# Block 0's feed-forward with VectorE in program order, and the last two groups' second layer inside the first pair of products

## The chip, the core and the metric

One NeuronCore of a Trainium2 chip runs the whole program. TensorE multiplies matrices into PSUM, VectorE and ScalarE work elementwise, GpSimd does a few subtractions and SyncE issues most DMA transfers. Each engine takes its own instructions in the order in which they stand, and semaphores join the engines. The metric is the device time of one execution in microseconds; lower is better.

## The reference, cut to what matters

```python
x = attention(q, k, v)                        # 8 batches of 576 tokens, chunks of 64 -> 4608 tokens of 512
gate = sigmoid(causal_depthwise_conv(x, conv_w))
y = (gate * (x @ w_val)) @ w_out              # 512 x 512 each
mu, var = y.mean(-1), y.var(-1)
xn = (y - mu) / sqrt(var + 1e-6) * g_ln
out = y + relu(xn @ w_ch1) @ w_ch2            # 512 x 2048 and 2048 x 512
```

The weights arrive as float64, and a matmul takes fp32r operands (fewer bits than f32), so a weight is decoded from its bit pattern to f32 and then split into a high and a low part; a product is high*high + high*low + low*high.

## The kernel before

The 4608 tokens are nine blocks of 512. Attention, gate and the two projections of all blocks come first, in an order that a planner writes out. Then comes the feed-forward, whose hidden 2048 columns are 16 groups f of 128. Block 0's feed-forward is done directly, group by group, while the weights are still being decoded; blocks 1 to 8 follow in pairs of blocks, by a scheme of 7 products in place of 8 (`ff_pair`, one call for each pair of groups; "pair 0" below is its first call, for groups 0 and 1 of blocks 1 and 2).

Block 0's part is a loop over f. `ff1(0, f)` is the first layer: 12 matmuls (`psh`, L219), then ScalarE's relu writes the high half `hh` (L646) and VectorE the low half `hl` (L647). PSUM holds two `psh` tiles, so ff1(f) can't begin before `hl` of group f-2 has been read out. `ff2` is the second layer: 12 matmuls into four accumulators (`acc`, L662). It runs two groups behind ff1, later one. Groups 0 to 3 have their weights decoded before; `next_ff(f + 5)` in iteration f loads and decodes group f+5: for each of the two weights A (first layer) and B (second layer) ScalarE converts the upper word (L162), VectorE shifts (L163), sets the sign (L164) and adds the lower bits (L165), ScalarE writes the high half (L170) and GpSimd the low half by a subtraction (L171). Three L16x instructions on one tile are called a chain below. `ln_rows` takes the LayerNorm of two row tiles of block 1 (f = 1, 3, 5, 7; L603 to L615 on VectorE, L608 and L617 on ScalarE), `turn_rows` turns them on TensorE (L625, f = 4, 6, 8, 10).

After f = 12 `right_operands` splits the turned rows of blocks 1 and 2 into the right-hand operands b21, b11, b22, t1, t2, t3, t4 of the products (L669 high on ScalarE, L670 low and L738 differences on VectorE). `make_pair` builds the left-hand operands of a pair: sums of decoded weights on VectorE (L713 to L716), high halves on ScalarE (L669), low halves on GpSimd (L670, 128x256). In `ff_pair` a product is 6 matmuls (L802); `copy` (L818), `add` (L822) and `relu` (L813, L814) sit between the products, and the list `fill` holds TensorE pieces that run between products (in pair 0: block 0's ff2 of group 15; in a later pair: the second layer of the pair before, L776).

Around the changed place only TensorE has its order from the program (`manual_schedule`); the other engines' order there comes from a scheduler that goes by priority.

Of the kernel before, what the change touches and what calls it, by code (L numbers as in the profile page):

```python
# [8 lines left out]
F32 = mybir.dt.float32  # L9
# [85 lines left out]
def tile_chunk_attention_gated_mlp(ctx: ExitStack, tc: tile.TileContext, qk, v, w_val, conv_w, w_out, g_ln, w1, w2, out):  # L95
# [199 lines left out]
    def load_half(i):  # L295
        f, r = divmod(i, 2)
        t = wraw[i] = stg.tile([P, DM, 2], U32, tag="raw", name=f"raw{r + 1}", bufs=2)
        if r:
            nc.sync.dma_start(out=t, in_=w2[f * P:(f + 1) * P])
        else:  # L300
            nc.sync.dma_start(
                out=t.rearrange("p (c f) w -> p c (f w)", c=CT),
                in_=w1[:, f * P:(f + 1) * P].rearrange("(c p) f w -> p c (f w)", p=P),
            )

    def plan_weights():
# [327 lines left out]
    def ff1(j, f):  # L634
# [6 lines left out]
        m = f % 3 if f <= NF - 4 else f % 2  # L641
        pool = p2["h3" if m == 2 else "h"]
        a = pool.tile([P, BLK], F32R, tag=f"hh{m}", name="hh", bufs=1)
        b = pool.tile([P, BLK], F32R, tag=f"hl{m}", name="hl", bufs=1)
        with tc.high_priority():
# [6 lines left out]
    def ff2(j, f):  # L652
        a, b = hh.pop((j, f))
        h2, l2 = w2s[f]
        if f == 0:
            for t in range(BLK // P):
                acc[t] = p2["acc"].tile([P, DM], F32, tag=f"acc{t}", name="acc")
        for t in range(BLK // P):
            ts = slice(t * P, (t + 1) * P)
            ops = [(a[:, ts], h2), (a[:, ts], l2), (b[:, ts], h2)]  # L660
            for i, (lt, rh) in enumerate(ops):
                nc.tensor.matmul(out=acc[t], lhsT=lt, rhs=rh, start=(f == 0 and i == 0), stop=(f == NF - 1 and i == 2))  # L662
        if f == NF - 1:
            for t in range(BLK // P):
                nc.vector.tensor_tensor(out=yt0[:, t, :], in0=acc.pop(t), in1=yt0[:, t, :], op=ALU.add)
                nc.sync.dma_start(out=rows(-1, t)[1], in_=yt0[:, t, :])

# [59 lines left out]

    def right_operands():

        xt = p2["xt"]  # L730
        b11, b12, b21, b22 = (xt[:, c:c + 2, t:t + BLK] for c in (0, 2) for t in (0, BLK))

        def make(nm, b):
            t = xb[nm] = p2["xb"].tile([P, 2, 2, BLK], F32R, tag=nm, name=nm)
            high_low(t[:, 0], t[:, 1], b, nc.vector)

        def sub(out, a, b, op=ALU.subtract):
            nc.vector.tensor_tensor(out=out, in0=a, in1=b, op=op)  # L738

        make("b21", b21)  # L740
        make("b11", b11)
        make("b22", b22)
        t3, t1, t2, t4 = b22, b12, b11, b21
        sub(t3, b22, b12)
        sub(t1, b12, b11)
        make("t1", t1)
        sub(t2, t3, b11, ALU.add)
        make("t2", t2)
        make("t3", t3)
        sub(t4, b21, t2)  # L750
        make("t4", t4)

# [36 lines left out]
    def ff_pair(s, p, fill):  # L789
# [3 lines left out]
        h = {}  # L793
        first = s == 0 and p == 0

# [35 lines left out]
        add(c)  # L831
        if not first:
            relu((0, 0), c)
        run(0, 3)
        if first:
            relu((0, 0), c)
        prod(zy, 2, "t1", True)
# [22 lines left out]
    def prep():  # L860
# [4 lines left out]
        pX = ctx.enter_context(tc.tile_pool(name="p2x", bufs=1, side="right", reuse_waits="tile"))  # L865
        p2["xt"] = pX.tile([P, CT, 2 * BLK], F32, name="xt")
        p2["0"] = s_0.enter_context(tc.tile_pool(name="p2a", bufs=1, side="right", reuse_waits="tile"))
        p2["h"] = s_0.enter_context(tc.tile_pool(name="p2h", bufs=2, side="right", reuse_waits="tile"))
        p2["acc"] = ctx.enter_context(tc.tile_pool(name="acc", bufs=1, space=PSUM, reuse_waits="tile"))
        xn0 = [p2["0"].tile([P, CT, BLK], F32R, name=f"xn{i}") for i in range(2)]  # L870
        yt0 = p2["0"].tile([P, HB, DM], F32, name="yt0")
        y0 = y_dram[0].rearrange("(t p) d -> p t d", p=P)
        nc.sync.dma_start(out=yt0, in_=y0)
        with tc.high_priority():
            ln_rows([yt0[:, i, :] for i in range(HB)])
        turn_rows([yt0[:, i, :] for i in range(HB)], 0)
# [20 lines left out]
    with tc.manual_schedule(engines={mybir.EngineType.PE, mybir.EngineType.DVE, mybir.EngineType.Activation, mybir.EngineType.Pool, mybir.EngineType.SP}):  # L897
        for name, at in plan.run():
# [35 lines left out]
    next_ff(NFA)  # L934
    ys = {0: pair_rows(0)}
    for f in range(NF):
        ff1(0, f)
        if f in (4, 6, 8, 10):
            turn_rows(ys.pop(f - 4), f - 4)
        if f > NF - 4:  # L940
            ff2(0, f - 1)
        elif f > 1:
            ff2(0, f - 2)
        if f == NF - 4:
            ff2(0, f - 1)
        if f in (1, 3, 5, 7):
# [15 lines left out]
    def open_rest():
        ff2(0, NF - 1)
        s_0.close()
        p2["hr"] = ctx.enter_context(tc.tile_pool(name="p2r", bufs=5, side="right", reuse_waits="tile"))
        p2["wx"] = ctx.enter_context(tc.tile_pool(name="p2w", bufs=1, side="right", reuse_waits="tile"))
        p2["yt"] = ctx.enter_context(tc.tile_pool(name="pyt", bufs=2, reuse_waits="tile"))

    fill = [open_rest]
    for s in range(NS):  # L970
# [51 lines left out]
```

## Time and profile before

| what | value |
|---|---|
| median of 3 runs | 1099.89 us (1098.13 to 1100.52) |
| profiled execution, its own time | 1100.13 us |
| its span | 1098.4 us |
| mean granted TensorE clock | 0.989 |
| TensorE busy | 1063.4 us (97%) |
| VectorE busy | 693.2 us (63%) |
| ScalarE busy | 496.3 us (45%) |
| GpSimd busy | 107.2 us (10%) |

Times in the trace count from the start of the span; the profiled execution's time is 1.7 us longer than its span. Block 0's feed-forward begins at 312.54, pair 0 follows it from about 410, and the later pairs fill the rest. In a row, the figure in brackets is the idle time of the engine just before the instruction, and behind the arrow stands what ended it.

### The profile page before, as it was taken

To read this page: it belongs to the slowest core of one execution; us is meant where nothing else is said; L and a number is where in the kernel's file an instruction comes from. 1 tells how busy PE (TensorE), PEld (TensorE's weight loads), DVE (VectorE), ACT (ScalarE), POOL (GpSimd) and SP (SyncE) were. 2 spreads that over 40 slices of the span, in tenths; PEclk is the share of its full clock that TensorE was granted. 3 is DMA by queue.
4 is the path that set the end of the run, shared out by engine and by line. 5 is a ranking of instruction groups with operands and counts; after the bars stand their busy time and mean duration, and the time that the engine had idled before them with its cause. 6 is when DMAs were issued, how large, how long until landed. Compare 5 with 4: busy or idle time off the path is not lost.

```text
span 1098.4 us, 17083 instructions
## 1 busy us (share of the span) xinstructions
PE 1063.4 (97%) x6858; PEld 863.1 (79%) x6858; DVE 693.2 (63%) x1153; ACT 496.3 (45%) x844; POOL 107.2 (10%) x120
## 2 busy tenths in 40 slices
PE   7799999999999898999999999999999999999998
PEld 7677778777777786888887888888788888788787
DVE  6899998999859885555457244448335438333434
ACT  3887787675847644245433134333233423212221
POOL 2110101010024433222200000000000000000000
PEclk9899999999999999999999999999999999999999
DMA  9544535433348626334426333324433223522202
GB/s 378 199 145 165 192 132 192 150 106 126 107 139 279 218 91 221 115 117 149 176 77 222 114 106 114 117 96 171 155 96 114 88 86 139 194 78 96 81 35 77
DMA packets 58581, 155.28 MB, mean 141 GB/s; under 512 B 5742, under 2 KB 13958, under 8 KB 56198
## 3 DMA queue, kind: packets, MB, share of 16 engines
q1 hardware_dynamic: 53318, 144.75, 37.9%
q10 hardware_dynamic: 5184, 9.44, 2.2%
q8 instruction: 54, 0.88, 0.3%
q14 instruction: 25, 0.20, 0.1%
HBM read 116.41 MB, written 37.75 MB: 140 GB/s over the span
## 4 chain that ended last, share of the span: by engine, by line
PE 72%; DVE 11%; ACT 5%; issue 3%; DMA 1%; POOL 1%; ACTq 0%; SPq 0%; DVEq 0%; POOLq 0%
PE acc L776 16%; PE x L802 15%; PE psf L776 15%; PE zy L802 10%; PE pso L566 5%; PE psv L533 4%; DVE cg L492 2%; PE acc L662 2%; DVE da L164 1%; DVE h L814 1%; PE x L408 1%; PE psh L219 1%; DVE da L165 1%; PE pst L625 1%; DMA raw<-in_moe_w_ch 1%
## 5 line engine op out<-in xcount | busy, mean ns | idle before, releaser
L822 DVE TENSOR_TENSOR c<-x,c 128x512 f32<-128x512 f32 x96 | 66.3, 690 | 238.5 <-ACT c L818 181.8
L776 PE MATMUL acc<-w,h 128*128 128x512 f32 x768 | 186.0, 391 | 0.0
L776 PE MATMUL psf<-w,h 128*128 128x512 f32 x768 | 186.0, 391 | 0.0
L776 PEld LDWEIGHTS acc<-w,h 128*128 128x128 f32 x768 | 144.2, 188 | 31.4
L776 PEld LDWEIGHTS psf<-w,h 128*128 128x128 f32 x768 | 144.2, 188 | 31.3
L802 PE MATMUL x<-t,wc 128*128 128x512 f32 x576 | 148.1, 393 | 3.4 <-DVE c L822 3.4
L818 ACT ACTIVATE c<-zy 128x512 f32<-128x512 f32 x96 | 58.0, 604 | 188.1 <-PE zy L802 188.0
L802 PEld LDWEIGHTS x<-t,wc 128*128 128x128 f32 x576 | 108.8, 189 | 27.8 <-DVE c L822 4.6
L813 ACT ACTIVATE h<-c 128x512 fp32r<-128x512 f32 x96 | 60.5, 631 | 135.9 <-DVE c L822 135.4
L781 DVE TENSOR_TENSOR yt<-psf,yt 128x512 f32<-128x512 f32 x128 | 88.2, 691 | 25.1 <-PE psf L776 21.1
L492 DVE SCALAR_TENSOR_TENSOR cg<-xf,cw,cg 128x516 f32<-128x516 f32 (+1 forms) x176 | 103.2, 651 | 0.0
L802 PE MATMUL zy<-b,wc 128*128 128x512 f32 x384 | 98.9, 393 | 0.0
L802 PEld LDWEIGHTS zy<-b,wc 128*128 128x128 f32 x384 | 71.2, 188 | 14.6
L814 DVE SCALAR_TENSOR_TENSOR h<-c,h 128x512 fp32r<-128x512 f32 x96 | 68.5, 714 | 13.4 <-ACT h L813 13.2
L533 PE MATMUL psv<-xh,vh 128*128 128x512 f32 x144 | 58.8, 409 | 2.8 <-DVE gv L543 2.0
L566 PE MATMUL pso<-oh,gh 128*128 128x512 f32 x144 | 59.3, 412 | 2.2 <-DVE gv L543 1.2
L566 PE MATMUL pso<-ol,gh 128*128 128x512 f32 x144 | 56.5, 393 | 1.3 <-POOL ol L262 1.3
L533 PE MATMUL psv<-xl,vh 128*128 128x512 f32 x144 | 56.6, 393 | 0.9 <-ACT xl L447 0.9
L533 PE MATMUL psv<-xh,vl 128*128 128x512 f32 x144 | 56.6, 394 | 0.0
L566 PE MATMUL pso<-oh,gl 128*128 128x512 f32 x144 | 56.0, 392 | 0.0
L813 ACT ACTIVATE h<-x 128x512 fp32r<-128x512 f32 x32 | 19.2, 600 | 81.0 <-PE x L802 81.0
L670 POOL TENSOR_TENSOR wc<-raws,wc 128x256 fp32r<-128x256 f32 x56 | 45.3, 831 | 106.1 <-ACT wc L669 99.6
(117 smaller groups left out, 1579.4 us busy)
## 6 DMA issues: line engine op xcount, KB each, us to landing
wc<-wc SPq DMA_DIRECT2D x112, 512.0 KB, 3.2
qkr<-in_qk SPq DMA_DIRECT2D x18, 1024.0 KB, 6.9
raw<-in_moe_w_ch SPq DMA_DIRECT2D x32, 512.0 KB, 4.2
vr<-in_v SPq DMA_DIRECT2D x18, 512.0 KB, 4.1
yd<-y ACTq DMA_DIRECT2D x36, 256.0 KB, 2.0
out<-yt SPq DMA_DIRECT2D x36, 256.0 KB, 3.7
yr<-yd SPq DMA_DIRECT2D x32, 256.0 KB, 3.1
yt<-yd SPq DMA_DIRECT2D x32, 256.0 KB, 3.9
```

The lines of the kernel that those rows point to most:

```text
L492: nc.vector.scalar_tensor_tensor(out=out, in0=xf[j][:, f, i + lo:i + hi], scalar=cw[:, i * CT + f:i * CT + f + 1], in1=out, op0=ALU.mult, ...
L533: nc.tensor.matmul(out=x["v", f], lhsT=lt[:, fs], rhs=rh[j][:, c, :], start=(c == 0 and k == 0), stop=(c == CT - 1 and k == 2))
L566: nc.tensor.matmul(out=x["o", t], lhsT=lt[j, f][:, ts], rhs=rh, start=(f == 0 and k == 0), stop=(f == CT - 1 and k == 2))
L662: nc.tensor.matmul(out=acc[t], lhsT=lt, rhs=rh, start=(f == 0 and i == 0), stop=(f == NF - 1 and i == 2))
L670: eng.tensor_tensor(out=lo, in0=a, in1=hi, op=ALU.subtract)
L776: nc.tensor.matmul(out=ps, lhsT=lt, rhs=rh, start=(g == 0 and k == 0 and (first or half)), stop=(g == 1 and k == 2 and (last or half)),)
L781: nc.vector.tensor_tensor(out=yt[i], in0=ps, in1=yt[i], op=ALU.add)
L802: nc.tensor.matmul(out=ps, lhsT=lt, rhs=rh, start=(start and c == 0 and i == 0), stop=(c == 1 and i == 2), skip_group_check=True)
L813: nc.scalar.activation(out=t[:, 0, :], in_=src, func=ACTF.Relu)
L814: nc.vector.scalar_tensor_tensor(out=t[:, 1, :], in0=src, scalar=0.0, in1=t[:, 0, :], op0=ALU.max, op1=ALU.subtract)
L818: nc.scalar.activation(out=t, in_=zy, func=ACTF.Copy)
L822: nc.vector.tensor_tensor(out=t, in0=x, in1=t, op=ALU.add)
```

## The change

In block 0's feed-forward VectorE, too, gets its order from the program, up to `order.close()` ahead of `ff_pair`; the LayerNorm there loses its high priority. `right_operands` becomes a list of eleven steps, four of which run after each of ff1(13), ff1(14) and ff1(15). ff2(14) and ff2(15) become eight pieces (`ff2_rows`) in the fill list of pair 0, where before one entry held ff2(15) whole; `relu((0, 0))` now stands ahead of the first pieces. Block 0's rows for the residual are loaded again at f = 12 into two smaller tiles. The h tiles hold both halves and share tags with the weight ring. `load_ff` of group 4 is called directly behind `prep`.

```diff
@@ -639,9 +639,9 @@
-        pool = p2["h3" if m == 2 else "h"]
-        a = pool.tile([P, BLK], F32R, tag=f"hh{m}", name="hh", bufs=1)
-        b = pool.tile([P, BLK], F32R, tag=f"hl{m}", name="hl", bufs=1)
+        pool, tag = (p2["h3"], "h2") if m == 2 else (p2["wx"], f"x{NFA + m}")
+        t = pool.tile([P, 2, 2, 2 * P], F32R, tag=tag, name="hh").rearrange("p a b w -> p a (b w)")
+        a, b = t[:, 0], t[:, 1]
@@ -650,20 +650,21 @@
     def ff2(j, f):
-        a, b = hh.pop((j, f))
+        for t in range(BLK // P):
+            ff2_rows(j, f, t)
+
+    def ff2_rows(j, f, t):
+        a, b = hh[j, f]
...
+        ops = [(a[:, ts], h2), (a[:, ts], l2), (b[:, ts], h2)]
+        for i, (lt, rh) in enumerate(ops):
+            nc.tensor.matmul(out=acc[t], lhsT=lt, rhs=rh, start=(f == 0 and i == 0), stop=(f == NF - 1 and i == 2))
         if f == NF - 1:
...
+            nc.vector.tensor_tensor(out=yt0[t], in0=acc.pop(t), in1=yt0[t], op=ALU.add)
+            nc.sync.dma_start(out=rows(-1, t)[1], in_=yt0[t])
@@ -726,6 +727,10 @@
     def right_operands():
+        for fn in right_steps():
+            fn()
+
+    def right_steps():
@@ -737,18 +742,13 @@
+        return [
+            lambda: make("b21", b21), lambda: make("b11", b11), lambda: make("b22", b22),
+            lambda: sub(t3, b22, b12), lambda: sub(t1, b12, b11), lambda: make("t1", t1),
+            lambda: sub(t2, t3, b11, ALU.add), lambda: make("t2", t2), lambda: make("t3", t3),
+            lambda: sub(t4, b21, t2), lambda: make("t4", t4),
+        ]
@@ -829,11 +828,8 @@
-        if not first:
-            relu((0, 0), c)
+        relu((0, 0), c)
         run(0, 3)
-        if first:
-            relu((0, 0), c)
@@ -907,6 +909,7 @@
     prep()
+    load_ff(NFA, stg)
@@ -917,12 +920,13 @@
-    order.enter_context(tc.manual_schedule(engines={mybir.EngineType.PE}))
+    order.enter_context(tc.manual_schedule(engines={mybir.EngineType.PE, mybir.EngineType.DVE}))
@@ -933,40 +937,44 @@
         ff1(0, f)
+        for fn in steps[:4]:
+            fn()
+        steps = steps[4:]
...
         if f > NF - 4:
-            ff2(0, f - 1)
+            if f < NF - 1:
+                ff2(0, f - 1)
...
         if f == NF - 4:
             ff2(0, f - 1)
+            first_rows()
...
-            with tc.high_priority():
-                ln_rows(ys[f - 1])
+            ln_rows(ys[f - 1])
...
-            right_operands()
+            steps = right_steps()
+    s_0.close()
+    p2["hr"] = ctx.enter_context(tc.tile_pool(name="p2r", bufs=5, side="right", reuse_waits="tile"))
     load_pair(0)
     load_pair(1)
     make_pair(0)
     load_pair(2)
...
+    order.close()
+    order.enter_context(tc.manual_schedule(engines={mybir.EngineType.PE}))
+
+    fill = [lambda f=f, t=t: ff2_rows(0, f, t) for f in (NF - 2, NF - 1) for t in range(HB)]
```

How this stands in the engines' queues is shown at three places. The line numbers of the changed kernel are one higher from L670 to about L740, and differ by a few after that.

VectorE, start of block 0's groups, the kernel before. `hl_3820`, `hl_3858` and `hl_3919` are the low halves of groups 0, 1 and 2; `da_3898` and `da_4016` are weights B of group 4 and A of group 6.

```order
L163 TENSOR_SCALAR da_3898<-da_3898 128x512
L164 SCALAR_TENSOR_TENSOR da_3898<-raw2_3886,da_3898 128x512
L647 SCALAR_TENSOR_TENSOR hl_3820<-psh_3806,hh_3819 128x512
L165 SCALAR_TENSOR_TENSOR da_3898<-raw2_3886,da_3898 128x512
L163 TENSOR_SCALAR da_4016<-da_4016 128x512
L164 SCALAR_TENSOR_TENSOR da_4016<-raw1_4011,da_4016 128x512
L603 BN_STATS s6_3865<-yr_3803 128x6
L647 SCALAR_TENSOR_TENSOR hl_3858<-psh_3844,hh_3857 128x512
L604 BN_AGGR mv_3864<-s6_3865 128x2
L603 BN_STATS s6_3868<-yr_3803 128x6
L647 SCALAR_TENSOR_TENSOR hl_3919<-psh_3905,hh_3918 128x512
```

The same place in the changed kernel. `hh_3823` and `hh_3860` are the tiles of groups 0 and 1, `da_3831` and `da_3840` are weights A and B of group 5.

```order
L647 SCALAR_TENSOR_TENSOR hh_3823<-psh_3810,hh_3823 128x512
L163 TENSOR_SCALAR da_3831<-da_3831 128x512
L164 SCALAR_TENSOR_TENSOR da_3831<-raw1_3826,da_3831 128x512
L165 SCALAR_TENSOR_TENSOR da_3831<-raw1_3826,da_3831 128x512
L163 TENSOR_SCALAR da_3840<-da_3840 128x512
L164 SCALAR_TENSOR_TENSOR da_3840<-raw2_3828,da_3840 128x512
L165 SCALAR_TENSOR_TENSOR da_3840<-raw2_3828,da_3840 128x512
L647 SCALAR_TENSOR_TENSOR hh_3860<-psh_3847,hh_3860 128x512
L603 BN_STATS s6_3867<-yr_3807 128x6
```

Group 5's two chains stand between the low halves of groups 0 and 1, where before they stood elsewhere and group 1's low half was followed directly by group 2's; from here on each iteration is one low half, the LayerNorm where there is one, and two whole chains.

ScalarE at the same point of the program, the changed kernel. `hh_3920` is the relu of group 2, `da_3900` weight B of group 6.

```order
L162 ACTIVATE da_3900<-raw2_3888 128x512
L646 ACTIVATE hh_3823<-psh_3810 128x512
L170 ACTIVATE w0_3790<-da_3791 128x512
L646 ACTIVATE hh_3860<-psh_3847 128x512
L646 ACTIVATE hh_3920<-psh_3907 128x512
L162 ACTIVATE da_3831<-raw1_3826 128x512
L162 ACTIVATE da_3840<-raw2_3828 128x512
```

The conversions L162 that group 5's chains need stand behind the relu of group 2.

VectorE at pair 0, the changed kernel. `hh_4659` is group 15's tile; `c_4722` is pair 0's `add` behind product 1; `raws_4673` and `raws_4674` hold pair 0's sums, `raws_4677` and `raws_4679` pair 1's.

```order
L671 TENSOR_TENSOR t2_4631<-xt_3540,t2_4631 128x1024
L647 SCALAR_TENSOR_TENSOR hh_4659<-psh_4646,hh_4659 128x512
L671 TENSOR_TENSOR t3_4662<-xt_3540,t3_4662 128x1024
L743 TENSOR_TENSOR xt_3540<-xt_3540 128x2x512
L821 TENSOR_TENSOR c_4722<-x_4715,c_4722 128x512
L717 TENSOR_TENSOR raws_4677<-raws_4677,raws_4679 128x256
L671 TENSOR_TENSOR t4_4666<-xt_3540,t4_4666 128x1024
L714 TENSOR_TENSOR raws_4674<-raws_4673 128x256
L813 SCALAR_TENSOR_TENSOR h_4731<-c_4722,h_4731 128x512
L715 TENSOR_TENSOR raws_4673<-raws_4673 128x256
L716 TENSOR_TENSOR raws_4674<-raws_4673 128x256
L717 TENSOR_TENSOR raws_4674<-raws_4673,raws_4674 128x256
```

In the kernel before, pair 0's four sums stand ahead of the low half of group 12, and the rows between group 15's low half (`hl_4674`) and the same `add` (`c_4735`) are these, of pairs 1 (`raws_4693`) and 2 (`raws_4724`).

```order
L670 TENSOR_TENSOR t2_4592<-xt_3540,t2_4592 128x1024
L738 TENSOR_TENSOR xt_3540<-xt_3540 128x2x512
L647 SCALAR_TENSOR_TENSOR hl_4674<-psh_4660,hh_4673 128x512
L670 TENSOR_TENSOR t4_4599<-xt_3540,t4_4599 128x1024
L716 TENSOR_TENSOR raws_4693<-raws_4693,raws_4695 128x256
L713 TENSOR_TENSOR raws_4724<-raws_4723 128x256
L714 TENSOR_TENSOR raws_4723<-raws_4723 128x256
L715 TENSOR_TENSOR raws_4724<-raws_4723 128x256
L716 TENSOR_TENSOR raws_4724<-raws_4723,raws_4724 128x256
L822 TENSOR_TENSOR c_4735<-x_4728,c_4735 128x512
```

So pair 0's sums moved from well ahead of pair 0 to behind its `add`, and t3's and t4's low halves with them.

## Rows read from the trace of the kernel before

**Rows 1.** Windows: stretch, its us, PE, PEld, DVE, ACT, POOL busy (count), clock, DMA

```profile
340.00:350.00 10.00, 10.00 (x49) 8.21 (x48) 9.79 (x21) 5.93 (x15) 4.21 (x3) 1.00 0.88 295
```

**Rows 2.** Timeline of TensorE, block 0's groups

```profile
323.80 2.50 PE L219 MATMUL psh<-xn,w 128*128 128x512 f32 x10
...
334.59 1.36 PE L625 MATMUL pst<-ident,yr 128*128 128x128 f32 x8 [2.27 <-ACT yr L617]
...
338.52 2.96 PE L219 MATMUL psh<-xn,w 128*128 128x512 f32 x12
...
350.56 1.79 PE L219 MATMUL psh<-xn,w 128*128 128x512 f32 x7
...
368.10 2.97 PE L219 MATMUL psh<-xn,w 128*128 128x512 f32 x12
...
383.82 4.51 PE L219 MATMUL psh<-xn,w 128*128 128x512 f32 x12 [3.52 <-DVE hl L647]
...
393.75 2.49 PE L219 MATMUL psh<-xn,w 128*128 128x512 f32 x10
```

**Rows 3.** Timeline of TensorE, pair 0 and the start of pair 1

```profile
422.90 2.93 PE L802 MATMUL x<-t,wc 128*128 128x512 f32 x6 [2.66 <-DVE c L822]
426.61 1.65 PE L802 MATMUL x<-t,wc 128*128 128x512 f32 x6 [0.78 <-DVE c L822]
...
430.80 1.43 PE L802 MATMUL x<-b,wc 128*128 128x512 f32 x5 [1.16 <-DVE h L814]
```

**Rows 4.** Timeline of TensorE, the LayerNorm of block 0

```profile
280.12 0.66 PE L625 MATMUL pst<-ident,yt 128*128 128x128 f32 x4 [1.19 <-ACT yt L617]
```

**Rows 5.** Timeline of ScalarE

```profile
321.24 0.60 ACT L646 ACTIVATE hh<-psh 128x512 fp32r<-128x512 f32 x1 [1.02 <-PE psh L219]
321.73 0.66 ACT L162 ACTIVATE da<-raw 128x512 f32<-128x512 f32 x1
...
408.46 1.05 ACT L669 ACTIVATE t<-xt 128x1024 fp32r<-128x1024 f32 x1
409.41 0.71 ACT L669 ACTIVATE wc<-raws 128x256 fp32r<-128x256 f32 x2
```

**Rows 6.** Timeline of VectorE

```profile
325.30 0.41 DVE L163 TENSOR_SCALAR da<-da 128x512 uint32<-128x512 uint32 x1
325.74 0.69 DVE L164 SCALAR_TENSOR_TENSOR da<-raw,da 128x512 uint32<-128x512 uint32 x1
326.47 1.67 DVE L165 SCALAR_TENSOR_TENSOR da<-raw,da 128x512 uint32<-128x512 uint32 x1
...
401.20 1.21 DVE L670 TENSOR_TENSOR t<-xt,t 128x1024 fp32r<-128x1024 f32 x1
```

**Rows 7.** Groups of VectorE by shape, 316 to 390: busy us, mean ns

```profile
L164 DVE SCALAR_TENSOR_TENSOR da<-raw,da 128x512 uint32<-128x512 uint32 x21 | 19.3, 922 | 0.2
L165 DVE SCALAR_TENSOR_TENSOR da<-raw,da 128x512 uint32<-128x512 uint32 x21 | 18.0, 861 | 0.2
...
L647 DVE SCALAR_TENSOR_TENSOR hl<-psh,hh 128x512 fp32r<-128x512 f32 x12 | 8.2, 680 | 0.2
L603 DVE BATCH_NORM_STATS2 s<-yr 128x6 f32<-128x512 f32 x8 | 5.3, 676 | 0.1
...
L612 DVE TENSOR_TENSOR w<-w,ve 128x2 f32<-128x2 f32 x4 | 0.6, 147 | 0.0
```

**Rows 8.** One line's instructions over the span, L164 and L171

```profile
L164 DVE SCALAR_TENSOR_TENSOR da<-raw,da x24: 674/684/1777, 258.2 to 387.4; 128x512 uint32<-128x512 uint32 x24
...
L171 POOL TENSOR_TENSOR w<-da,w x24: 1287/1338/2634, 314.1 to 389.7; 128x512 fp32r<-128x512 f32 x24
```

**Rows 9.** Timeline of GpSimd

```profile
326.05 1.54 POOL L171 TENSOR_TENSOR w<-da,w 128x512 fp32r<-128x512 f32 x1 [4.41 <-ACT w L170]
...
351.09 5.60 POOL L171 TENSOR_TENSOR w<-da,w 128x512 fp32r<-128x512 f32 x3 [1.36 <-ACT w L170]
```

**Rows 10.** The page's costliest groups: GpSimd's low halves for the products

```profile
L670 POOL TENSOR_TENSOR wc<-raws,wc 128x256 fp32r<-128x256 f32 x56 | 45.3, 831 | 106.1 <-ACT wc L669 99.6
```

More of the change, by code (lines that the diff above doesn't have):

```diff
@@ L296, in load_half @@
         f, r = divmod(i, 2)
-        t = wraw[i] = stg.tile([P, DM, 2], U32, tag="raw", name=f"raw{r + 1}", bufs=2)
+        t = tiles["rf", i] = stg.tile([P, DM, 2], U32, tag="raw", name=f"raw{r + 1}", bufs=2)
         if r:
@@ L328, in hi_lo @@
                 return tiles["hl", "f", i]
-            plan_decode(("f", i), lambda i=i: wraw[i], hi_lo, [("raw", "f", i), ("lo", ("vo"[1 - r], f))], 2000 + i, store=None if r else a_dram[f])
+            plan_decode(("f", i), lambda i=i: tiles["rf", i], hi_lo, [("raw", "f", i), ("lo", ("vo"[1 - r], f))], 2000 + i, store=None if r else a_dram[f])
         def turn():
@@ L652, in ff2 @@
     def ff2(j, f):
-        a, b = hh.pop((j, f))
+        for t in range(BLK // P):
+            ff2_rows(j, f, t)
+    def ff2_rows(j, f, t):
+        a, b = hh[j, f]
         h2, l2 = w2s[f]
         if f == 0:
[L656 to L662, printed above, removed]
+            acc[t] = p2["acc"].tile([P, DM], F32, tag=f"acc{t}", name="acc")
+        ts = slice(t * P, (t + 1) * P)
+        ops = [(a[:, ts], h2), (a[:, ts], l2), (b[:, ts], h2)]
+        for i, (lt, rh) in enumerate(ops):
+            nc.tensor.matmul(out=acc[t], lhsT=lt, rhs=rh, start=(f == 0 and i == 0), stop=(f == NF - 1 and i == 2))
         if f == NF - 1:
-            for t in range(BLK // P):
-                nc.vector.tensor_tensor(out=yt0[:, t, :], in0=acc.pop(t), in1=yt0[:, t, :], op=ALU.add)
-                nc.sync.dma_start(out=rows(-1, t)[1], in_=yt0[:, t, :])
+            nc.vector.tensor_tensor(out=yt0[t], in0=acc.pop(t), in1=yt0[t], op=ALU.add)
+            nc.sync.dma_start(out=rows(-1, t)[1], in_=yt0[t])
     def high_low(hi, lo, a, eng):
@@ L738, in sub @@
             nc.vector.tensor_tensor(out=out, in0=a, in1=b, op=op)
-        make("b21", b21)
-        make("b11", b11)
-        make("b22", b22)
         t3, t1, t2, t4 = b22, b12, b11, b21
[L744 to L751, printed above, removed]
+        return [
[4 more added lines that the diff above has]
+        ]
     yt = {}
@@ L793, in ff_pair @@
         h = {}
-        first = s == 0 and p == 0
         def prod(ps, k, nm, start):
@@ L866, in prep @@
         p2["xt"] = pX.tile([P, CT, 2 * BLK], F32, name="xt")
+        p2["wx"] = ctx.enter_context(tc.tile_pool(name="p2w", bufs=1, side="right", reuse_waits="tile"))
+        p2["yt"] = ctx.enter_context(tc.tile_pool(name="pyt", bufs=2, side="right", reuse_waits="tile"))
         p2["0"] = s_0.enter_context(tc.tile_pool(name="p2a", bufs=1, side="right", reuse_waits="tile"))
-        p2["h"] = s_0.enter_context(tc.tile_pool(name="p2h", bufs=2, side="right", reuse_waits="tile"))
         p2["acc"] = ctx.enter_context(tc.tile_pool(name="acc", bufs=1, space=PSUM, reuse_waits="tile"))
         xn0 = [p2["0"].tile([P, CT, BLK], F32R, name=f"xn{i}") for i in range(2)]
-        yt0 = p2["0"].tile([P, HB, DM], F32, name="yt0")
-        y0 = y_dram[0].rearrange("(t p) d -> p t d", p=P)
-        nc.sync.dma_start(out=yt0, in_=y0)
+        first_rows()
         with tc.high_priority():
-            ln_rows([yt0[:, i, :] for i in range(HB)])
-        turn_rows([yt0[:, i, :] for i in range(HB)], 0)
-        nc.sync.dma_start(out=yt0, in_=y0)
+            ln_rows(yt0)
+        turn_rows(yt0, 0)
         for i in range(0, HB, 2):
@@ L880, in prep, with first_rows @@
             high_low(xn0[0][:, :, ts], xn0[1][:, :, ts], p2["xt"][:, :, ts], nc.vector)
+    def first_rows():
+        nonlocal yt0
+        yt0 = []
+        for i in range(0, HB, 2):
+            t = p2["yt"].tile([P, 2, DM], F32, name="yt")
+            nc.sync.dma_start(out=t, in_=y_dram[0][i * P:(i + 2) * P, :].rearrange("(t p) d -> p t d", p=P))
+            yt0 += [t[:, k, :] for k in range(2)]
     plan_loads()
@@ L924, in next_ff @@
             pool = stg2 if f % 2 else stg
-            load_ff(f, pool)
+            if f not in wraw:
+                load_ff(f, pool)
             split_ff(f, pool)
@@ L935, in tile_chunk_attention_gated_mlp @@
     ys = {0: pair_rows(0)}
+    steps = []
     for f in range(NF):
         ff1(0, f)
+        for fn in steps[:4]:
+            fn()
+        steps = steps[4:]
         if f in (4, 6, 8, 10):
@@ L945, in tile_chunk_attention_gated_mlp @@
             ff2(0, f - 1)
+            first_rows()
         if f in (1, 3, 5, 7):
@@ L960, in tile_chunk_attention_gated_mlp @@
     load_pair(2)
[L962 to L969, printed above, removed]
+    for fn in steps:
+        fn()
+    order.close()
+    order.enter_context(tc.manual_schedule(engines={mybir.EngineType.PE}))
+    fill = [lambda f=f, t=t: ff2_rows(0, f, t) for f in (NF - 2, NF - 1) for t in range(HB)]
     for s in range(NS):
```

## The prediction

> **What bounds the kernel now.** I read the page's busy times first, then the windows over block 0's feed-forward, then TensorE's timeline for its waits there, and behind each wait the timelines of the engine that ended it. TensorE is busy 97% of the span, so over the whole kernel only what makes TensorE stand still can be won or lost. Block 0's feed-forward is different: between 340 and 350 TensorE is busy 10.00 us of 10 and VectorE 9.79 [rows 1]. Two engines are full at once there, and whichever has more work per group sets the pace.
>
> TensorE's losses between 280 and 431 are few and can be counted: 1.19 in the LayerNorm of block 0 [rows 4], 2.27 and 3.52 in the groups [rows 2], 2.66 and 0.78 in pair 0 and 1.16 at the start of pair 1 [rows 3]. Behind a long wait the matmuls themselves take longer: twelve took 4.51 behind the 3.52, where twelve take 2.96 at 338.52 [rows 2], 1.55 more; six took 2.93 behind the 2.66, against 1.48, half of a 2.96 [rows 2, 3]. With no loss a group takes TensorE 5.6 (two layers of 2.8); two groups with one turn of the rows took 338.52 to 350.56, that is 12.04 [rows 2].
>
> **The change, part by part.** The span is 1098.4 and the profiled execution's own time 1100.13; the sum is made against the latter, which stands 0.24 above the median of 1099.89.
>
> *Prep: -0.8.* The 1.19 wait is for ScalarE's normalized rows of block 0 [rows 4]. In the changed order no decode of group 6 stands ahead of that LayerNorm on VectorE, so the wait should go, -1.2; but group 6's conversion on ScalarE stands where it can hold up the same rows until its weight has landed, so I give a part back. Bounds -1.2 and +0.4.
>
> *ff1(3): a new wait of 3.9.* ff1(3) needs the low half of group 1 read out of PSUM. Before, it began at 323.80 without a wait [rows 2]. Now group 5's two chains stand ahead of that low half, and their conversions L162 stand behind the relu of group 2. Group 2's first layer ended at 321.2, when its relu was released [rows 5]; less 0.8 this is 320.4. The relu takes 0.49 to the next instruction and L162 0.66 [rows 5]: 321.6. A chain is 0.44 (325.30 to 325.74) + 0.73 (to 326.47) + 0.63, the last from 0.68 less the overlap of one instruction with the next: 1.80 [rows 6, 7]. Two chains 3.6, one collision with GpSimd 1.0 (below), the low half 0.68 [rows 7]: 326.9. ff1(3) was due at 323.80 - 0.8 = 323.0, so it waits 3.9 and loses some 1.5 more by slow matmuls. VectorE goes on from 326.9: a LayerNorm 3.3 (two statistics of 0.6, nine or ten small steps of 0.15 to 0.2, some 0.4 for ScalarE's root; an estimate from [rows 7]), two chains 3.6, the low half of group 2 0.6: 334.4, which is also when ff1(4) can begin.
>
> *VectorE's rounds.* From there VectorE does per two groups four chains 7.2, two low halves 1.2 and a LayerNorm 3.3: 11.7. That is under TensorE's 12.04, but by 0.3 only. On top come collisions. L164 takes 0.684 in the median and up to 1.777 [rows 8]; L165 began at 326.47, while GpSimd's subtraction ran from 326.05 for 1.54, and took 1.67 [rows 6, 9]. So a collision costs VectorE 1.0. The cheapest reading is the mean over 21 instructions: 0.922 and 0.861 against 0.684, that is 0.42 per chain, 1.7 per round [rows 7, 8]; nothing at all if GpSimd is the one that gives way, as it did at 351.09, where three subtractions took 5.60, not 3 x 1.34 [rows 8, 9]; the dearest is four collisions, 4.0. I take three, 3.0: in the changed order a chain follows the other directly, so the subtraction of the first, which starts when ScalarE's high half is done, falls into the chain behind it; the scheduler's order of before put low halves and LayerNorm steps in between. A round is then 14.7, 2.7 over TensorE's.
>
> The Trainium skill (SBUF — State Buffer, "Who interferes with whom") says that a VectorE instruction with two SBUF inputs and a GpSimd instruction that reads SBUF lock each other out, and that the one issued later waits for the whole of the other. By that rule a collision could cost the whole of L171, 1.29 and not 1.0; three rounds would end 2.6 later and the time would be 1110.6. The trace agrees in kind (1.67 inside 1.54), and that a loss can fall on either engine is in the 5.60.
>
> Three rounds from the low half of group 2 to that of group 8: 334.4 + 44.1 = 378.5, when ff1(10) can begin; before it began at 368.10 [rows 2]. From there to ff1(13) before took 25.65, in which lie the 3.52 and the 1.55 [rows 2]; VectorE now has no LayerNorm left and keeps up, so 20.6, plus 0.9 for slow matmuls behind the last wait (between 0 and 1.55). ff1(13) begins at 400.0 instead of 393.75: **+6.2**, with prep in it. The 2.27 and the 3.52 are gone, but as waits on each low half they come back larger.
>
> *Pair 0: +2.9.* Now the splits of the right-hand operands stand in program order. Call E the end of ff1(15). Group 15's low half stands behind t2's low half, and that behind t2's high half on ScalarE, which stands behind the relu of group 15: E + 0.8 for the relu, 1.05 for the high half [rows 5], 1.21 for the low half [rows 6], 0.68 for group 15's: E + 3.65. Product 1 needs that PSUM tile and is due at E + 1.4: it waits 2.3, and some 0.3 for slower matmuls. Next, pair 0's four sums now stand behind the `add` of product 1, with a sum of pair 1 and t4's low half ahead of them. Product 2 needs the second sum, split. From the end T of product 1: `add` 0.68, a sum 0.43, t4's low half 1.21, a sum 0.43, the relu's low half 0.68, the sum 0.43, ScalarE's copy 0.36 (half of 0.71), GpSimd 0.83 [rows 5, 6, 10], 5.05, and eight handovers of about 0.1: T + 5.9. (The sum is an estimate from half a 128x512 `add`.) TensorE has three pieces of the second layer to do meanwhile, 2.1 (a quarter of a layer, 0.7, each). It waits 3.8, with 1.4 for slow matmuls. Together 7.8. What pair 0 lost before, 2.66 + 1.45 + 0.78 = 4.9 [rows 3], is covered now by the pieces that stand later. Difference +2.9; bounds -3 (pieces and sums fall well) and +5.
>
> *Pair 1: -1.2.* The 1.16 wait [rows 3] is for a low half that stood behind LayerNorm rows; the relu no longer has them ahead.
>
> *At nothing:* the h tiles' new place, the rows loaded at f = 12 (their next use is the last `add` of block 0, tens of us later), `load_ff` moved forward (its issue is one of many on SyncE; if it holds a later load, 0.5). The matmuls are the same in number.
>
> Sum: +6.2 + 2.9 - 1.2 = +7.9; 1100.13 + 7.9 = **1108.0**.
>
> **The rivals.** *B: collisions cost what they cost before.* 1.7 per round: round 13.4, three rounds end 3.9 earlier and the one at ff1(3) is smaller too; ff1(13) at 395.8, +2.1; with +2.9 - 1.2: **1103.9**. For it the means of 21 instructions each; against it that VectorE then had other work between chains.
>
> *C: not slower, GpSimd gives way.* The place is the round: if a collision stretches L171 and not VectorE, as at 351.09 [rows 9], VectorE's round is 11.7, TensorE's 12.04 decides, and the point is 0.34 of collisions per round. ff1(4) at 333.4, six groups with three turns 36.0, ff1(10) at 369.4, +20.6 and about 1.1: ff1(13) at 391.1, -2.65. With pair 0 and pair 1: 1100.13 - 2.65 + 2.9 - 1.2 = **1099.2**, no measurable change. *D: faster*, if pair 0 also loses only as much as before or less (the sums' chain is covered by pieces): 1099.2 - 2.9 to - 5 = **1095**. Against both: L164's 1.777 and L165's 1.67.
>
> *E: later still.* The decoded weights are stored and raw weights loaded by SyncE behind the chains; with VectorE later, the loads of the next groups are issued later, and a group's conversion could wait for its weight as well. Some 1.5 per round twice: over **1113**.
>
> **How the numbers follow.** Forecast A .53, B .18, C .11, D .10, E .08. The predicted time is that of A, which by itself runs from 1105 to 1113. The range leaves out D and E's upper part: 1098.0 to 1113.5. A measurement of this kernel can tell about 0.2%, 2.2 us. Faster is D, .10; same is C, .11; slower is A, B and E, .79.
>
> **What would show it.** In the profile after: a wait of 3 to 5 ahead of ff1(3) and one ahead of most first layers from ff1(4) to ff1(10), all ended by VectorE's low half; L164 and L165 means over 0.9; ff1(13) near 400; in pair 0 a wait of about 2.3 ahead of product 1 and 3 to 4 ahead of product 2; none at pair 1's product 1. VectorE idle for more than 1 us per round ahead of chains would speak for E, first layers without waits for C. I am wrong if the scheduler's interleaving of before cost as many collisions as the program order does, or if the collisions of a round fall on GpSimd.

## The result and the profile after

The changed kernel takes 1109.81 us (median of 4 runs, 1109.47 to 1114.25) against 1099.56 of before on the same chip; the ratio is 1.0104, with a 95% interval of 1.0076 to 1.0132. It is slower, as forecast, 10.2 us by the medians where 7.9 were forecast; the time lies inside the range. The profiled execution took 1109.61 with a span of 1107.6, against 1100.13 and 1098.4: 9.2 us of span, which are looked for below.

TensorE's timeline of the changed kernel over block 0's groups (start, length, ..., in brackets the wait ahead of it and what ended it) answers to [rows 2]:

```profile
326.08 4.61 PE L219 MATMUL psh<-xn,w 128*128 128x512 f32 x12 [3.72 <-DVE hh L647]
333.50 3.07 PE L219 MATMUL psh<-xn,w 128*128 128x512 f32 x12
...
349.19 4.58 PE L219 MATMUL psh<-xn,w 128*128 128x512 f32 x12 [2.64 <-ACT w L170]
...
363.60 3.07 PE L219 MATMUL psh<-xn,w 128*128 128x512 f32 x12 [0.66 <-DVE hh L647]
...
378.10 3.07 PE L219 MATMUL psh<-xn,w 128*128 128x512 f32 x12 [2.24 <-DVE hh L647]
...
399.64 2.96 PE L219 MATMUL psh<-xn,w 128*128 128x512 f32 x12
```

These are ff1(3), (4), (6), (8), (10) and (13). The forecast had ff1(3) at 326.9 behind 3.9 of waiting, ff1(10) at 378.5 and ff1(13) at 400.0. The profile puts the 2.64 at 349.19 down to a weight's high half, which ended at 349.11, but that weight belongs to a later group; the low half that ff1(6) needs ended at 349.05 (VectorE, below). Behind the waits of 3.72 and 2.64 the twelve matmuls take 4.6, at a granted clock of 0.62; behind the 2.24 they take 3.07, at 1.00.

VectorE's timeline of the changed kernel from ahead of the low half of group 4 to that of group 6 shows a round, that is VectorE's work for two groups:

```profile
346.80 1.65 DVE L165 SCALAR_TENSOR_TENSOR da<-raw,da 128x512 uint32<-128x512 uint32 x1
348.37 0.68 DVE L647 SCALAR_TENSOR_TENSOR hh<-psh,hh 128x512 fp32r<-128x512 f32 x1
...
349.41 1.66 DVE L164 SCALAR_TENSOR_TENSOR da<-raw,da 128x512 uint32<-128x512 uint32 x1
...
352.89 1.66 DVE L165 SCALAR_TENSOR_TENSOR da<-raw,da 128x512 uint32<-128x512 uint32 x1
...
361.28 1.67 DVE L165 SCALAR_TENSOR_TENSOR da<-raw,da 128x512 uint32<-128x512 uint32 x1
362.87 0.68 DVE L647 SCALAR_TENSOR_TENSOR hh<-psh,hh 128x512 fp32r<-128x512 f32 x1
```

GpSimd's timeline of the changed kernel over the same time:

```profile
346.44 1.45 POOL L171 TENSOR_TENSOR w<-da,w 128x512 fp32r<-128x512 f32 x1 [4.34 <-ACT w L170]
349.19 1.33 POOL L171 TENSOR_TENSOR w<-da,w 128x512 fp32r<-128x512 f32 x1 [1.29 <-ACT w L170]
352.54 1.47 POOL L171 TENSOR_TENSOR w<-da,w 128x512 fp32r<-128x512 f32 x1 [2.02 <-ACT w L170]
...
360.92 1.47 POOL L171 TENSOR_TENSOR w<-da,w 128x512 fp32r<-128x512 f32 x1 [4.33 <-ACT w L170]
```

From the low half at 348.37 to that at 362.87, two groups on, are 14.50, of which three instructions of 1.66 or so, each begun 0.2 to 0.4 after a subtraction, take 0.97 more than the 0.69 of an undisturbed one. The round was put at 14.7 with three collisions of 1.0. Over all chains between 312 and 400 the groups of VectorE by shape read, in the changed kernel (behind the bar: busy us, mean ns, and idle us before them):

```profile
L165 DVE SCALAR_TENSOR_TENSOR da<-raw,da 128x512 uint32<-128x512 uint32 x22 | 23.9, 1085 | 0.7
L164 DVE SCALAR_TENSOR_TENSOR da<-raw,da 128x512 uint32<-128x512 uint32 x22 | 20.1, 914 | 0.8
```

[rows 7] had 861 for L165 and 922 for L164. TensorE's timeline of the changed kernel from pair 0 on answers to [rows 3]:

```profile
417.32 2.05 PE L801 MATMUL x<-b,wc 128*128 128x512 f32 x6 [2.17 <-DVE hh L647]
419.16 3.45 PE L664 MATMUL acc<-w,hh 128*128 128x512 f32 x9
424.45 0.73 PE L801 MATMUL zy<-t,wc 128*128 128x512 f32 x2 [1.84 <-ACT wc L670]
425.46 2.07 PE L801 MATMUL zy<-t,wc 128*128 128x512 f32 x4 [0.28 <-POOL wc L671]
...
433.51 1.66 PE L801 MATMUL x<-t,wc 128*128 128x512 f32 x6 [0.61 <-DVE c L821]
...
439.35 1.65 PE L801 MATMUL x<-b,wc 128*128 128x512 f32 x6
...
460.68 1.66 PE L801 MATMUL x<-b,wc 128*128 128x512 f32 x6 [0.47 <-DVE h L813]
```

Product 1 waits 2.17 for group 15's low half, product 2 waits 1.84 and 0.28 for its split sum; the three pieces between took 3.45 and not 2.1, so slow matmuls stand where part of that second wait would be (the granted clock is 0.91 from 400 to 440, and 0.72 from 417.3 to 429.3). A wait of 0.61 for an `add` follows at 433.51. Pair 1's product 1, at 439.35, does not wait any more. The account: ff1(13) 5.89 later (399.64 against 393.75), from there to pair 1's product 1 39.71 instead of 37.05, 2.66 more, and 0.65 behind it, 0.47 of that the wait at 460.68; together the 9.2 of the spans.

### The profile page after: what moved, and what is told of

The parts are those of the page before. It is cut to its first block, busy times and chain, and to the rows that moved or that the text cites. A ratio compares the mean times of both kernels' runs of the same rounds, so it can differ in the third digit from the quotient of the medians.

```text
span 1107.6 us, 17091 instructions
## 1 busy us (share of the span) xinstructions
PE 1067.9 (96%) x6858; PEld 864.8 (78%) x6858; DVE 699.9 (63%) x1153; ACT 497.3 (45%) x844; POOL 106.1 (10%) x120
## 4 chain that ended last, share of the span: by engine, by line
PE 72%; DVE 10%; ACT 5%; issue 4%; DMA 1%; POOL 1%; ACTq 0%; SPq 0%; DVEq 0%; POOLq 0%
PE acc L776 16%; PE x L801 15%; PE psf L776 14%; PE zy L801 10%; PE pso L566 7%; PE psv L533 5%; DVE da L164 2%; DVE h L813 1%; PE x L408 1%; PE pst L625 1%; DVE cg L492 1%; DVE da L163 1%; PE psh L219 1%; DVE yt L781 1%; ACT cg L518 1%
## 5 line engine op out<-in xcount | busy, mean ns | idle before, releaser
L813 DVE SCALAR_TENSOR_TENSOR h<-c,h 128x512 fp32r<-128x512 f32 x96 | 67.7, 705 | 10.3 <-ACT h L812 10.2
L219 PE MATMUL psh<-xn,w 128*128 128x512 f32 x192 | 51.0, 419 | 9.8 <-DVE hh L647 7.1
```

Source lines behind the costliest of these rows:

```text
L219: nc.tensor.matmul(out=ps, lhsT=lt, rhs=rh, start=(i == 0), stop=(i == n - 1))
L813: nc.vector.scalar_tensor_tensor(out=t[:, 1, :], in0=src, scalar=0.0, in1=t[:, 0, :], op0=ALU.max, op1=ALU.subtract)
```

## The experiments

The theory: VectorE's program order costs in two places, ahead of the low halves of block 0's groups, with GpSimd's subtractions stretching the chains, and ahead of pair 0's second operand. The rivals: the other edits (pieces, tiles, loads) cost; the waiting in order itself costs, not the collisions; or VectorE's whole queue is late, so that a wait removed at one place comes back at another. The table gives for each profiled execution the start of ff1(13) and of pair 1's product 1 and the span, and the median of its runs with the ratio to the kernel before. Each ratio is to runs of the kernel before that were made beside it: their median was 1100.75 for the first four experiments, 1100.57 for the next four and 1101.53 for the last three.

| kernel | ff1(13) | pair 1, product 1 | span | median | ratio (95%) |
|---|---|---|---|---|---|
| before | 393.75 | 430.80 | 1098.4 | 1099.56 | 1 |
| changed | 399.64 | 439.35 | 1107.6 | 1109.81 | 1.0104 (1.0076 to 1.0132) |
| VectorE to the scheduler | 391.07 | 422.41 | 1090.1 | 1092.16 | 0.9919 (0.9895 to 0.9942) |
| before, with the order | 399.07 | 436.52 | 1104.2 | 1106.76 | 1.0049 (1.0025 to 1.0072) |
| no subtraction | 391.90 | 431.93 | 1101.1 | 1102.87 (one run) | |
| decode later | 392.64 | 437.05 | 1108.3 | 1109.95 | 1.0076 (1.0050 to 1.0101) |
| sums early | 399.71 | 435.64 | 1103.4 | 1105.26 | 1.0039 (1.0024 to 1.0054) |
| t2 behind | 400.15 | 440.60 | 1109.0 | 1112.02 | 1.0104 (1.0089 to 1.0119) |
| order until f = 12 | 399.11 | 430.86 | 1098.7 | 1101.32 | 1.0010 (0.9998 to 1.0022) |
| scheduler, no pieces | 391.55 | 425.19 | 1093.1 | 1094.65 | 0.9942 (0.9927 to 0.9957) |
| scheduler, LayerNorm first | 392.88 | 424.19 | 1092.2 | 1094.01 | 0.9926 (0.9904 to 0.9947) |
| scheduler, turn later | 396.08 | 427.57 | 1095.5 | 1096.01 | 0.9944 (0.9922 to 0.9966) |
| scheduler, both | 393.70 | 425.07 | 1093.0 | 1094.97 | 0.9942 (0.9922 to 0.9962) |

**VectorE given back to the scheduler.**

```diff
-    order.enter_context(tc.manual_schedule(engines={mybir.EngineType.PE, mybir.EngineType.DVE}))
+    order.enter_context(tc.manual_schedule(engines={mybir.EngineType.PE}))
```

> The changed kernel with VectorE's order given back to the scheduler (only TensorE in program order); the pieces, the h tiles, the late rows and the steps stay. If VectorE's program order is what costs, both ahead of group 1's low half and in the rounds, ff1(13) begins near 393.5 instead of 399.64, pair 0's sums stand early again and product 2 does not wait; some wait of 1 to 2 us ahead of product 1 stays, as the pieces no longer cover it: 1098 to 1102 us. If instead the pieces, the tiles or the moved loads cost, it stays above 1105.

It is 0.8% faster than the kernel before, further than expected. Against the changed kernel the one line is worth 17.5 us of span, 8.57 of them before ff1(13) and 8.37 from there to pair 1. TensorE's timeline of this kernel:

```profile
335.42 1.97 PE L625 MATMUL pst<-ident,yr 128*128 128x128 f32 x8 [4.34 <-ACT yr L617]
...
391.07 2.96 PE L219 MATMUL psh<-xn,w 128*128 128x512 f32 x12
...
422.41 1.65 PE L801 MATMUL x<-b,wc 128*128 128x512 f32 x6
```

One wait of 4.34 for the first normalized rows is left in the groups, and none behind it: neither on a low half nor in pair 0. So the other edits don't cost; together they win 8.3 us of span against the kernel before: 1.2 ahead of the groups, 1.4 in them and 5.7 from ff1(13) to pair 1. The expected wait ahead of product 1 did not come: group 15's low half, at 405.92, stands behind t2 there too, but VectorE reaches it in time.

**The order alone, in the kernel before.** VectorE's program order and the LayerNorm without priority, until f = 12.

```diff
+    order.enter_context(tc.manual_schedule(engines={mybir.EngineType.PE, mybir.EngineType.DVE}))
...
         if f == NF - 4:
+            order.close()
+            order.enter_context(tc.manual_schedule(engines={mybir.EngineType.PE}))
```

> The kernel before with one part of the change alone: VectorE in program order, and the LayerNorm without priority, from the start of block 0's groups until the right-hand operands (behind f = 12). If the order alone costs, ff1(3) waits 3 to 4, ff1(13) begins 6 to 8 later than 393.75, pair 0 is as before (34.3 us): 1105 to 1108. If the order costs only together with the other edits: under 1102.

1106.76, as the theory has it: the same 3.72 ahead of ff1(3), and ff1(13) at 399.07. The order costs without the other edits.

**No subtraction.** GpSimd writes zeros in its place and reads nothing.

```diff
-        nc.gpsimd.tensor_tensor(out=lo, in0=a, in1=hi, op=ALU.subtract)
+        nc.gpsimd.memset(lo.bitcast(F32), 0.0)
```

> The changed kernel, in which GpSimd writes zeros as the low halves of the weights of groups 4 to 15 in block 0 instead of subtracting (the low parts of these weights are left out): GpSimd then reads nothing. If collisions with GpSimd's subtraction make VectorE's round longer than TensorE's, no L164 or L165 takes over 0.75, a round is 11.7 to 12.1, ff1(3) waits about 2.8 and ff1(13) begins near 391: about 1101. If VectorE's own waiting in order makes the round, ff1(13) stays behind 397: over 1106. If writing alone collides too, L165 keeps some 1.6.

The groups of VectorE by shape, 312 to 400, in this kernel:

```profile
L164 DVE SCALAR_TENSOR_TENSOR da<-raw,da 128x512 uint32<-128x512 uint32 x22 | 15.2, 693 | 0.8
L165 DVE SCALAR_TENSOR_TENSOR da<-raw,da 128x512 uint32<-128x512 uint32 x22 | 15.2, 692 | 0.7
```

and TensorE's timeline:

```profile
325.57 3.06 PE L219 MATMUL psh<-xn,w 128*128 128x512 f32 x12 [2.97 <-DVE hh L647]
333.40 4.60 PE L219 MATMUL psh<-xn,w 128*128 128x512 f32 x12 [2.00 <-DVE hh L647]
...
371.46 3.07 PE L219 MATMUL psh<-xn,w 128*128 128x512 f32 x12 [0.25 <-DVE hh L647]
...
391.90 2.96 PE L219 MATMUL psh<-xn,w 128*128 128x512 f32 x12
```

No chain instruction is long any more, the waits ahead of ff1(3) and ff1(4) stay (the chains still stand ahead of the low halves), and after them TensorE runs almost without a wait: the round is TensorE's again and ff1(13) begins at 391.90 where 391 was expected. Up to ff1(13) the collisions are worth 7.7 us, by one run; VectorE's waiting in order is not what makes the round. (That the weights are ready earlier here is no gain by itself: in the changed kernel no wait of TensorE was for GpSimd's part of them.) The memsets also don't wait for ScalarE's high half and were through by 329, so this run does not tell whether writing alone collides. Pair 0, in which GpSimd still subtracts, keeps its waits.

**Each group decoded one iteration later.**

```diff
-        next_ff(f + NFA + 1)
+        if f:
+            next_ff(f + NFA)
```

> The changed kernel with each group decoded one iteration later (group 5 behind group 1's low half, and so on). Two chains less stand ahead of each low half. If VectorE's queue ahead of the low halves is what delays TensorE, ff1(3) begins without a wait near 322.3, ff1(10) near 367.5 although a round of VectorE stays 14.5, ff1(13) at 388 to 391: 1098 to 1101. If the sum of VectorE's work binds wherever it stands, ff1(3)'s wait is given back in the rounds and ff1(13) stays behind 396: over 1105.

A miss for the theory as it was put. TensorE's timeline of this kernel:

```profile
322.45 2.96 PE L219 MATMUL psh<-xn,w 128*128 128x512 f32 x12
...
371.52 3.04 PE L219 MATMUL psh<-xn,w 128*128 128x512 f32 x12 [0.73 <-ACT w L170]
...
413.91 2.92 PE L801 MATMUL x<-b,wc 128*128 128x512 f32 x6 [4.34 <-DVE hh L647]
...
421.88 0.73 PE L801 MATMUL zy<-t,wc 128*128 128x512 f32 x2 [1.81 <-ACT wc L670]
```

ff1(3) begins at 322.45 without a wait, as expected, and ff1(13) at 392.64, 7.0 earlier than in the changed kernel. But TensorE then meets VectorE's late queue in pair 0: product 1 waits 4.34 instead of 2.17, and at pair 1's product 1 only 2.3 are left; a wait of 1.93 at 459.83 in pair 2 takes the rest. What stands in VectorE's queue up to product 2 comes late here too, and the theory needs this rival in it. Whether that is for want of VectorE's time or because of its order, this run does not tell; the run with the order only until f = 12, below, does.

**Pair 0's sums early**: `load_pair(0)`, `load_pair(1)` and `make_pair(0)` at f = 12.

```diff
+            load_pair(0)
+            load_pair(1)
+            make_pair(0)
             steps = right_steps()
```

> The changed kernel with pair 0's rows loaded and its sums made at f = 12, ahead of the steps. If product 2 waits because the sums stand behind the add, its wait (1.84 and 0.28) and the slow matmuls behind it go, the 2.17 ahead of product 1 stays, pair 0 falls from 38.1 to 33 or 34: 1104.5 to 1106.5. If VectorE's queue as a whole is what is late there, the four sums only move the lateness ahead: over 1108.

1105.26, inside the expected band. Product 2 doesn't wait; product 1 waits 3.14 (expected 2.17); the sums now stand ahead of its low half. Against the changed kernel the move wins 4.2 us of span.

**t2 behind the low half of group 15.**

```diff
-        for fn in steps[:4]:
+        n = 3 if f == NF - 2 else 4
+        for fn in steps[:n]:
```

> The changed kernel with three steps behind ff1(14) in place of four, so that t2's split stands behind group 15's low half. The 2.17 ahead of product 1 goes or falls under 0.5. If the waits of pair 0 are separate, the time falls by 2 to 2.5: about 1107.5. If product 2 is bound by what VectorE's queue holds up to the sums, the same work still stands ahead of it and the wait goes to product 2: 1109 to 1110.

TensorE's timeline of this kernel:

```profile
424.90 3.09 PE L801 MATMUL zy<-t,wc 128*128 128x512 f32 x6 [5.44 <-ACT wc L670]
```

Product 1's wait goes, and product 2 begins at 424.90, where it began at 424.45 before this edit: the whole wait went there. Product 2 is bound by what stands in VectorE's queue up to the sums, not by the place of one split. It is even a little slower than expected (1112.02), with slow matmuls behind the longer wait.

**The order only until f = 12.**

```diff
         if f == NF - 4:
+            order.close()
+            order.enter_context(tc.manual_schedule(engines={mybir.EngineType.PE}))
             s_1.close()
```

> The changed kernel with VectorE in program order only until f = 12 and left to the scheduler from the steps on. If the losses of pair 0 come from the order there, ff1(13) stays at 399 to 400 and pair 0 takes 30 as with the scheduler: 1100 to 1103. If they come from VectorE being late already, pair 0 stays at 36 or more: over 1106.

ff1(13) stays at 399.11, the only wait left in pair 0 is 0.46, and the kernel is level with that of before. So the two places cost about the same: 8.6 us of span in the groups (against the scheduler's 1090.1; 8.04 of it up to ff1(13)) and 8.9 in pair 0 and behind it, and the second is not a mere consequence of the first. VectorE's timeline of the changed kernel, at the low half of group 13:

```profile
403.27 0.69 DVE L647 SCALAR_TENSOR_TENSOR hh<-psh,hh 128x512 fp32r<-128x512 f32 x1 [3.73 <-ACT hh L646]
403.88 3.49 DVE L671 TENSOR_TENSOR b<-xt,b 128x1024 fp32r<-128x1024 f32 x3
```

VectorE's in this kernel:

```profile
400.70 3.48 DVE L671 TENSOR_TENSOR b<-xt,b 128x1024 fp32r<-128x1024 f32 x3
404.11 0.68 DVE L647 SCALAR_TENSOR_TENSOR hh<-psh,hh 128x512 fp32r<-128x512 f32 x1
```

and TensorE's:

```profile
415.07 1.66 PE L801 MATMUL x<-b,wc 128*128 128x512 f32 x6 [0.46 <-DVE hh L647]
...
418.64 1.54 PE L801 MATMUL zy<-t,wc 128*128 128x512 f32 x6
```

In the program order VectorE stands idle 3.73 until group 13's relu is done, and 1.13 and 1.26 more for ScalarE's high halves of t1 and t2, while splits and sums stand behind in its queue; ScalarE had the high halves of the first three splits done at 401.2. Left to the scheduler, VectorE takes sums and these three splits in that time and has no wait between 391.1 and 415.0, and product 2 begins without a wait. So in pair 0 VectorE is not short of time: its order makes it idle, and the same work fits with ff1(13) as late.

**The scheduler's order without the pieces.** In the loop ff2(14) again, behind product 1 ff2(15) whole.

```diff
-            if f < NF - 1:
-                ff2(0, f - 1)
+            ff2(0, f - 1)
...
+    fill = [lambda: ff2(0, NF - 1)]
```

> The kernel of the first run (VectorE left to the scheduler) without the pieces: ff2(14) in the loop and ff2(15) whole behind product 1, as in the kernel before. If the pieces are what takes pair 0 from 34.3 to 29.8, it returns to 34 and the time to 1096 to 1098. If relu((0, 0)) ahead of the fill or the tiles did it, it stays under 1094.5.

1094.65, between the two bands and below what was expected of the pieces: they are worth 2.5 us by the medians, not 4.5. Waits of 1.41 and 0.78 for the `add` return, the first of them shorter than the 2.66 of [rows 3]; the relu that now stands ahead of the fill is a likely reason for that, but no run has it alone.

**The wait for the first normalized rows**, in the scheduler's order: the LayerNorm's priority put back; each turn of rows behind the second layer of its iteration; both.

```diff
-            ln_rows(ys[f - 1])
+            with tc.high_priority():
+                ln_rows(ys[f - 1])
```

> The kernel of the first run (VectorE left to the scheduler, 1092.2) with the LayerNorm's priority put back, as in the kernel before. Its one wait left in the groups, 4.34 ahead of the first turned rows, is for the LayerNorm; if its place in VectorE's and ScalarE's queues is the cause, the wait falls to 2.3 or less: 1089.5 to 1091. If VectorE's work as a whole is what is late, a low half takes the wait over, as at 383.82 before: 1092 or more.

> The kernel of the first run with each turn of rows behind the second layer of its iteration in place of ahead of it: 2.8 us of matmuls stand between. The 4.34 falls to about 1.6 and the slow turn behind it (1.97 where others take 1.04) with it: 1088.5 to 1090. If the lost time returns as a wait on a low half: 1092.

> Both edits. If the wait is all there is to win, it goes entirely: 1087 to 1089. If the LayerNorm's priority delays decodes or low halves, no better than the better of the two.

None is faster than 1092.16. For the first and the third that is the second case of the expectation, in which the wait only moves; the second, at 1096.01, lies above both of its cases. TensorE's timeline with the priority:

```profile
334.75 1.97 PE L625 MATMUL pst<-ident,yr 128*128 128x128 f32 x8 [2.27 <-ACT yr L617]
...
390.48 2.56 PE L664 MATMUL acc<-w,hh 128*128 128x512 f32 x10 [2.43 <-DVE hh L647]
```

The 4.34 falls to 2.27 as expected, and 55 us later a low half takes 2.43. With the turn later the 4.34 falls to 1.62, and low halves take 2.04 and 2.02; with both it is gone, and four first layers wait 0.74 to 2.51. That VectorE's work as a whole is the bound in the scheduler's order too is not shown: with VectorE left to the scheduler and none of these edits, VectorE is busy 31.0 of the 37.0 us from 341 to 378, and TensorE all of them. With the priority, the late low half, at 389.74, stands behind seven sums for the pairs and a chain, from 384.42 on, so its place in the order is as likely a reason. (The groups also begin 1.4 to 1.7 later in the first two of these kernels, at 312.69 and 312.97 against 311.30; why is open.)

## Why the prediction was right

*Prep.* Put at -0.8; the 1.19 wait went [rows 4] and nothing was given back: the groups begin at 310.93 instead of 312.54, -1.6; where the 0.4 beyond the 1.19 comes from is open. The doubt about group 6's conversion was not borne out.

*ff1(3).* 3.72 where 3.9 stood, at 326.08 instead of 326.9; that the conversions stand behind the relu of group 2 is in VectorE's idle time of 5.09 ahead of its first chain at 320.81. Two steps of the LayerNorm and no chain stood between the low halves of groups 1 and 2 in the kernel before, so the one did not quite follow the other directly.

*The rounds.* 14.50 from 348.37 to 362.87 where 14.7 stood, and 14.50 for the next; the first, from 332.77, took 15.60, with four long instructions. One of these was L163 at 335.15, 1.52 instead of 0.42, which the prediction did not count among those that collide. Three rounds are 44.6 where 44.1 stood. The waits that they bring stand ahead of ff1(5), (6), (8) and (10), 0.51 to 2.64: four of seven first layers where most were forecast. Of rivals B (13.4) and C (11.7) the trace shows neither, nor E: between 329 and 390 VectorE did not wait for a conversion. Without the subtraction (C's premise, no loss on VectorE, made true) ff1(13) came to 391.90, where C had 391.1. In the round shown one collision costs 0.97, and not all of L171. By the Trainium skill (SBUF — State Buffer, "Who interferes with whom") the later one waits for the whole of the other. The trace agrees to 0.1: the three began 0.22, 0.35 and 0.36 after a subtraction, and of an undisturbed 1.29 that leaves 1.07, 0.94 and 0.93. The 1.29 that the prediction worked out by that rule was too much because VectorE's instruction was not there from the start of the subtraction.

*ff1(13)*: +5.9 where +6.2 stood. That it is so near is partly luck: 0.8 more was won ahead of the groups than put, and the rounds took 0.5 more.

*Pair 0 and pair 1.* -1.16 at pair 1 came as forecast. Pair 0 was mis-sized: +2.66 with pair 1 in it where +1.7 stood. Product 1's 2.17 fits the 2.3 (the four terms of E + 3.65 add up to 3.74, which changes nothing). Product 2's chain took about as long as worked out: from the end of product 1, where the pieces begin at 419.16, 5.3 to product 2's first matmul and 6.3 to its third, which needs GpSimd's part; 5.9 in the sum. The waits in brackets, 1.84 and 0.28, are less than the 3.8 because slow pieces, 3.45 and not 2.1, filled most of the rest. Slow matmuls of the products cost a little more than put: product 1 took 2.05, the last four matmuls of product 2 2.07 and product 3 2.15. What the sum did not have is the wait of 0.61 at 433.51 for the second `add`: the prediction took all that pair 0 lost before as covered by the pieces. 0.65 behind pair 1, most of it the 0.47 at 460.68, was not in the sum at all. These two, 1.3 together, are what the span is longer by than the sum; they bring 1109.81 nearer to the 1110.6 of dearer collisions than to 1108.0, and the collisions themselves were not dearer.

What the prediction did not see is the size of the two halves. It wrote pair 0's gains from the pieces off against the new waits (4.9 lost before, 7.8 now); the scheduler's order shows that the other edits alone win 8.3 us of span and the order costs 17.5. In pair 0 it followed VectorE's order rightly from the end of ff1(15) on; that VectorE had stood idle 3.73 in that order before, with splits behind it, it did not count.

## What to carry to other kernels

Where two engines are both nearly full, moving one piece of work in the order of the busier one may only move a wait: here a wait taken away at one place came back at the next three times (decode later, t2 behind, LayerNorm first), while fewer collisions, or an order without idle time, shortened the kernel. So look at the busier engine's idle time too, and at what stood ready behind it in its queue. An order written by hand that puts whole dependent chains ahead of the instruction that frees a buffer costs that chain on the engine that waits for the buffer. Edits handed over together should be timed apart: here one line cost 17.5 us and hid 8.3 that the rest won.

## What the hardware showed

In the scheduler's order the collisions cost the chains less; some fall on small steps and on GpSimd. VectorE's groups by shape, 312 to 400, in the kernel with VectorE left to the scheduler:

```profile
L164 DVE SCALAR_TENSOR_TENSOR da<-raw,da 128x512 uint32<-128x512 uint32 x21 | 17.4, 834 | 0.2
L165 DVE SCALAR_TENSOR_TENSOR da<-raw,da 128x512 uint32<-128x512 uint32 x21 | 16.5, 795 | 0.1
```

and its GpSimd and VectorE timelines at the same time:

```profile
348.94 5.26 POOL L171 TENSOR_TENSOR w<-da,w 128x512 fp32r<-128x512 f32 x3 [6.26 <-ACT w L170]
```

```profile
348.79 0.68 DVE L165 SCALAR_TENSOR_TENSOR da<-raw,da 128x512 uint32<-128x512 uint32 x1
349.39 1.27 DVE L614 TENSOR_TENSOR r<-r,w 128x2 f32<-128x2 f32 x1
```

The L165 at 348.79 begins 0.15 ahead of the first subtraction and takes its usual 0.68; a step on two columns, L614, 0.16 in the median, begins behind it and takes 1.27; and the three subtractions take 5.26 instead of three times 1.29, which is 3.9. So both sides lose here. In the program order one L16x starts about 0.03 after the end of the one it depends on, while independent ones overlap a little, and that gap may be where a subtraction gets in. That it decides the side that waits is not shown; no run varied it alone.
